# Chunk attention and a two-layer feed-forward on one core: q and k turned by transposing DMAs from the tenth group on

## The chip, the cores and the metric

The kernel runs on one core of a Trainium2 chip. The metric is the device time of one execution in microseconds (us). The kernel before took 294.09 us, the median of three runs (294.02 to 294.42).

## The reference

Attention within chunks of 64 tokens, then a feed-forward layer with a leaky ReLU. Inputs and output are float32; the kernel works in float16 with float32 sums.

```
# q, k, v: (8 batches, 8 heads, 576 tokens, 64); chunk = 64, so 9 chunks a batch
scores = (1/sqrt(64)) * matmul(q_c, k_c.T)        # per batch, head and chunk: 64 x 64
scores = scores - max(scores, axis=-1)
attn   = exp(scores); attn = attn / (sum(attn, axis=-1) + 1e-9)
x      = matmul(attn, v_c)                        # laid out as (4608 tokens, 512)
h      = x @ w_in                                 # 512 -> 2048
g      = maximum(0.01 * h, h)
out    = g @ w_out                                # 2048 -> 512
```

## The kernel before, in words

**Groups.** The 4608 tokens are taken in 36 groups of 128 tokens (two chunks), numbered u. A group crosses the border of two batches where u is 13, 22 or 31 among the later ones. Each group goes through these stages, each of which is one function that takes u:

- q and k have to stand with the head dimension on the partitions. For groups 0 to 8 (u below UD = 9) they are loaded by rows of tokens (load_qk, L59) and turned by TensorE (stage_tq L260, stage_tk L265), then copied out by VectorE and ScalarE into QZ and KT (stage_q L270, stage_k L278). For groups 9 to 35 a whole batch is loaded at a time in pieces of 32 numbers (load_qk_batch L77, issue on L86, 8 DMAs for q and 8 for k, tiles q_d and k_d, two buffers each) and VectorE turns it in 32x32 blocks (stage_dq L287 with its instruction on L290, twice a group; stage_dk L295 with its instruction on L298).
- QZ holds q of two heads on the two halves of the partitions, with zeros beside them, so that one 128-row weight load gives both heads' scores. There are three QZ buffers, used in turn.
- stage_s (L303) makes the scores Sp: 8 matmuls with 64 columns. stage_m (L315) and stage_b (L319) take the maximum and subtract it on VectorE, stage_x (L325) is the exponential on ScalarE, stage_z and stage_n (L331, L339) sum, invert and scale on VectorE, giving the tile en.
- en is turned again, by TensorE for groups 0 to 8 (stage_e, stage_c) and by a transposing DMA on SP's queue for the later ones (stage_d L359, issue on L361), giving the tile et (four buffers).
- stage_v (L365) multiplies by v, giving xp, and stage_a copies it on ScalarE into xT (L385). stage_v also starts the load of v two batches ahead (load_v, issue on L95).

**Feed-forward.** Once the tokens of a block (128, 256 or 512) stand in xT, the block is cut into pieces that the function fill(n) takes in order: mm1 (hT, matmul on L155, each piece gives one PSUM bank; ScalarE makes gT of it on L170) and mm2 (oP, matmul on L180, a piece is 4 matmuls of 512 columns). After four mm2 pieces, store (L189) copies oP to osb (three buffers) on ScalarE and issues its DMA on SP's queue (L193). hT and oP share four PSUM banks.

**Order.** The program is scheduled by hand: each engine and each queue runs its instructions in the order in which the Python issues them. The first groups follow the list FRONT. Then one loop runs over `it` from 6 to 38. Iteration `it` does the scores of group it-1, the turning of q and k of group it, and the values of an older group, with feed-forward pieces between them:

```
    for it in range(6, NU + 3):
        stage_s(it - 1); stage_m(it - 1); stage_b(it - 1)
        if dve: stage_dq(it, 0)
        fill(2)
        stage_x(it - 1)
        ...
        if dve: stage_dq(it, 1); stage_dk(it)
        ...
        stage_z(it - 1); stage_n(it - 1); stage_d(it - 1)
        fill(2)
        values(it - 3)
        fill(3 if dve and it >= 17 else 2)
        if it == 9 * b // 2 - 4: load_qk_batch(b)
```

SP's queue carries stage_d's transposing DMAs and the output stores; POOL's (GpSimd's) queue carries all casting loads from float32 to float16, issued at first by the list LOADS (L131), whose last entry D2 loads q and k of batch 2. A DMA queue is in order too: what waits at its head holds back what is behind it.

Of the kernel before, what the change touches and what calls it, by code (L numbers as in the profile page):

```python
# [8 lines left out]
FP16 = mybir.dt.float16  # L9
# [7 lines left out]
def kernel(  # L17
# [9 lines left out]
    nc = tc.nc  # L27

    B, H, S, D = q.shape
# [3 lines left out]
    CH = 64  # L33
# [1 line left out]
    NT = d_model // 128  # L35
    NFC = d_ff // 128
    SCL = float(D) ** -0.5
    NQZ = 3
    NVB = 2
    NIN = 9  # L40
    UD = 9
    G = 2 * CH

    NU = n_tok // G
    BLOCKS = [128] * 6 + [256] + [128] * 2 + [256] * 5 + [512] * 4

    sbp = ctx.enter_context(tc.tile_pool(name="k_sb", bufs=1))
# [2 lines left out]


    VB = [sbp.tile([128, H // 2, NCH, 128], FP16, name=f"VB{i}") for i in range(NVB)]
    QZ = [sbp.tile([128, 4, 2, 2, CH], FP16, name=f"QZ{i}") for i in range(NQZ)]
    w_inT = sbp.tile([128, NT, d_ff], FP16, name="w_inT")
    w_outT = sbp.tile([128, NFC, d_model], FP16, name="w_outT")
    xT = sbp.tile([128, NT, n_tok], FP16, name="xT")
    qk: dict[int, tuple[bass.AP, bass.AP]] = {}

    def load_qk(u):  # L59
# [12 lines left out]
            both.append(t)  # L72
        qk[u] = tuple(both)

    qkd: dict[int, tuple[bass.AP, bass.AP]] = {}

    def load_qk_batch(b):  # L77
        both = []
        for name, src in (("q_d", q), ("k_d", k)):
            t = sbp.tile([128, 2, 2, S // 32, 32], FP16, name=name, tag=name, bufs=2)  # L80
            for m in range(2):
                for s in range(2):
                    for dh in range(2):
                        p0 = s * 64 + dh * 32
                        h0 = 4 * m + 2 * s
                        nc.gpsimd.dma_start(  # L86
                            out=t[p0:p0 + 32, m, :, :, :].rearrange("p h b d -> p (h b) d"),
                            in_=src[b, h0:h0 + 2, :, dh * 32:dh * 32 + 32].rearrange("h (b t) d -> t (h b) d", t=32),
                        )
            both.append(t.rearrange("p m h b d -> p (m h) (b d)"))  # L90
        qkd[b] = tuple(both)

    def load_v(b):
        for m in range(2):
# [25 lines left out]
    for eng, name, src in ((nc.sync, "q_f", q), (nc.scalar, "k_f", k)):  # L120
        t = sbp.tile([128, H, D], FP32, name=name)
# [7 lines left out]
    qk[0] = tuple(sbp.tile([128, H, D], FP16, name=n, tag=n, bufs=NIN) for n in ("q_in", "k_in"))  # L129

    LOADS = (  # L131
        "g1 v0 g2 Q0 Q1 g3 Q2 Q3 g4 P0 P1 P2 P3 g5 v1 g6 g7 g8 D2 "
    )
    LOADERS = {"g": load_qk, "v": load_v, "Q": load_w_in_quarter, "P": load_w_out_quarter, "D": load_qk_batch}
    ident = sbp.tile([128, 128], FP16, name="ident")
    for n, what in enumerate(LOADS.split()):
        LOADERS[what[0]](int(what[1:]))
        if n == 0:
# [91 lines left out]
    def fill(n):  # L230
        for _ in range(n):
            if not chunks:
                return
            kind, j, a, p = chunks[0]
            if START[j] + BLOCKS[j] > state["tokens"]:
                return
            chunks.pop(0)
            if kind == "mm1":
                mm1(j, a)
                act1(j, a)  # L240
            elif j == len(BLOCKS) - 1 and a == BLOCKS[j] // 128 - 1:
                if p == 0:
                    last(j, a)
            else:
                mm2(j, a, p)
                if parts[j, a] == NFC // 4:
                    store(j, a)
# [21 lines left out]

    def stage_q(u, s, act=0):  # L270
        part = slice(s * CH, (s + 1) * CH)
        to, of = QZ[u % NQZ][part, :, :, s, :], QP[u][part]
        if act:
            nc.scalar.activation(out=to, in_=of, func=AFT.Copy, bias=0.0, scale=1.0)
        else:
            nc.vector.tensor_copy(out=to, in_=of)

    def stage_k(u):  # L278
        KT[u] = sbp.tile([128, 4, 2, CH], FP16, name="KT", tag="KT", bufs=3)
        nc.scalar.activation(out=KT[u], in_=KP.pop(u), func=AFT.Copy, bias=0.0, scale=1.0)  # L280

    def cuts(u):
        r0, r1 = u * G, (u + 1) * G
        cut = min(-(-r0 // S) * S, r1) if r0 % S else r1
        return [(a // S, a % S, (a - r0) // CH, (z - a) // CH) for a, z in ((r0, cut), (cut, r1)) if a < z]

    def stage_dq(u, s):  # L287
        qz = QZ[u % NQZ]
        for b, at, e0, n in cuts(u):
            nc.vector.transpose(  # L290
                out=qz[s * CH:(s + 1) * CH, :, e0:e0 + n, s, :],
                in_=qkd[b][0][s * CH:(s + 1) * CH, :, at:at + n * CH].rearrange("p h (e t) -> p h e t", e=n),
            )

    def stage_dk(u):  # L295
        KT[u] = sbp.tile([128, 4, 2, CH], FP16, name="KT", tag="KT", bufs=3)
        for b, at, e0, n in cuts(u):
            nc.vector.transpose(  # L298
                out=KT[u][:, :, e0:e0 + n, :],
                in_=qkd[b][1][:, :, at:at + n * CH].rearrange("p h (e t) -> p h e t", e=n),  # L300
            )

    def stage_s(u):  # L303
        qz, kt = QZ[u % NQZ], KT.pop(u)
        Sp = psp.tile([128, 8, CH], FP32, name="Sp", tag="Sp", bufs=1)
        for i in range(8):
            g, e, m = i // 4, i // 2 % 2, i % 2
            nc.tensor.matmul(  # L308
                out=Sp[:, i, :], lhsT=qz[:, 2 * m + g, e, :, :], rhs=kt[:, 2 * m + g, e, :], start=True, stop=True
            )  # L310
        SP[u] = Sp

# [53 lines left out]
    def stage_v(u):  # L366
        et = ET.pop(u)
        xp = psp.tile([128, NT, 2, CH], FP32, name="xp", tag="ox", bufs=1)
        for e in range(2):
            b, c = divmod(2 * u + e, NCH)  # L370
            for t in range(NT):
                nc.tensor.matmul(  # L372
                    out=xp[:, t, e, :],
                    lhsT=VB[b % NVB][:, t, c, :],
                    rhs=et[:, t // 2, e, t % 2, :] if u < UD else et[:, t % 2, e, t // 2, :],
                    start=True,
                    stop=True,
                )
            if c == NCH - 1 and b + NVB < B:
                load_v(b + NVB)  # L380
        XP[u] = xp
# [33 lines left out]
    def empty(i):  # L415
        i, m = divmod(i, 2)
        return VB[i][m * CH:(m + 1) * CH, :, :, (1 - m) * CH:(2 - m) * CH]

    def zero(i):
        nc.vector.memset(QZ[i] if i < NQZ else empty(i - NQZ), 0.0)  # L420

    def zero_act(i):
        to = empty(i - NQZ)
        for t in range(2):
            part = to[:, 2 * t:2 * t + 2]
            p0 = (i - NQZ) % 2 * CH
            nc.scalar.activation(
                out=part,
                in_=zeros[p0:p0 + CH].unsqueeze(2).unsqueeze(3).to_broadcast(part.shape),
                func=AFT.Copy, bias=0.0, scale=1.0,  # L430
            )
# [8 lines left out]
    )  # L440
    STAGES = {
        "tq": stage_tq, "tk": stage_tk, "q": stage_q, "k": stage_k, "s": stage_s, "m": stage_m, "b": stage_b,
        "x": stage_x, "z": stage_z, "n": stage_n, "e": stage_e, "c": stage_c, "v": stage_v, "a": stage_a,
        "A": first_layer, "G": act1, "B": second_layer, "O": finish, "i": idle, "y": zero, "w": zero_act,
        "h": cast_q, "hk": cast_k,
    }
    for what in FRONT.split():
        name = what.rstrip("0123456789.")
        STAGES[name](*(int(x) for x in what[len(name):].split(".") if x))
    def values(u):  # L450
        if 3 < u < NU:
            stage_v(u)
            stage_a(u)

    for it in range(6, NU + 3):
        dve = UD <= it < NU
        if it <= NU:
            stage_s(it - 1)
            stage_m(it - 1)
            stage_b(it - 1)  # L460
        if dve:
            stage_dq(it, 0)
        fill(2)
        if it <= NU:
            stage_x(it - 1)
        if it - 2 < UD:
            stage_e(it - 2)
            stage_c(it - 2)
        if dve:
            stage_dq(it, 1)  # L470
            stage_dk(it)
        elif it < UD:
            stage_tq(it)
            stage_tk(it)
            stage_q(it, 0)
            stage_q(it, 1)
            stage_k(it)
        if it <= NU:
            stage_z(it - 1)
            stage_n(it - 1)  # L480
            if it - 1 >= UD:
                stage_d(it - 1)
        fill(2)
        values(it - 2 if it - 2 < UD else it - 3 if it - 3 >= UD else -1)
        fill(3 if dve and it >= 17 else 2)
        for b in range(3, B):
            if it == 9 * b // 2 - 4:
                load_qk_batch(b)
    fill(len(chunks))


# [28 lines left out]
```

## Time and profile before

| what | value |
|---|---|
| median of three runs | 294.09 us (294.02 to 294.42) |
| span of the profiled execution, first to last instruction | 292.1 us |
| median less span | 2.0 us |
| granted TensorE clock | 1.000 |
| TensorE (PE) busy | 283.5 us, 97% |
| VectorE (DVE) busy | 183.8 us, 63% |
| ScalarE (ACT) busy | 155.2 us, 53% |
| GpSimd (POOL) busy, mostly issuing loads | 119.5 us, 41% |
| SP's transposing DMAs et<-en | 27 |

The profile gives a span for the profiled execution and no time of its own beside it. Sums are therefore made on the span, and the 2.0 us between it and the median, which lie outside the first and the last instruction, are carried along.

How to read it: the page's first part gives each engine's busy time, its fourth the chain of work that ended last, followed back from the end, and its fifth the costliest groups of instructions with the idle time ahead of them and what ended it. A line such as "L290 DVE STREAM_TRANSPOSE QZ<-q_d" is line 290 of the kernel, on VectorE, writing QZ from q_d. "SPq" is SP's own instruction stream, which issues DMAs; a DMA's landing is when its data has arrived.

### The profile page before, as it was taken

Reading aid. Unit: us, or ns where it says so; the run is one execution under the profiler, and the core shown is the slowest. Engines: PE = TensorE matmul, PEld = TensorE weight load, DVE = VectorE, ACT = ScalarE, POOL = GpSimd, SP = SyncE. Lnnn points to the kernel's source line nnn. Section 1 sums busy time; section 2 is a strip of 40 time slices with the busy share of each in tenths; the row PEclk is TensorE's granted clock in tenths of the full one; section 3 lists DMA queues with packets and bytes.
Section 4 is the critical chain, followed back from the end, with each engine's and each line's share of the span. In section 5 each row is a group of like instructions: output and inputs, shape, how many; then the busy total and the mean of one; then the engine's idle time right before and its main releaser. Section 6 shows DMA issues by size and latency. Waiting matters only on the chain.

```text
span 292.1 us, 6233 instructions
## 1 busy us (share of the span) xinstructions
PE 283.5 (97%) x2564; PEld 181.0 (62%) x2564; DVE 183.8 (63%) x343; ACT 155.2 (53%) x268; POOL 119.5 (41%) x148
## 2 busy tenths in 40 slices
PE   4989999999999999999999999999999999999995
PEld 4979845888677766767676744444445444444444
DVE  6987417789899998777787788778876730000000
ACT  6457623666555555646564647734873377127511
POOL 8867547998408936913295369130000000000000
PEclk9999999999999999999999999999999999999999
DMA  9999999999969999999499399999111320120022
GB/s 132 169 193 193 203 157 198 151 148 144 124 97 96 162 78 158 154 142 90 101 107 132 61 159 147 78 65 163 54 20 54 73 91 0 38 81 28 0 74 72
DMA packets 192476, 32.00 MB, mean 110 GB/s; under 512 B 183488, under 2 KB 187968, under 8 KB 192448
## 3 DMA queue, kind: packets, MB, share of 16 engines
q0 software_dynamic: 170208, 18.10, 117.7%
q1 hardware_dynamic: 21056, 13.18, 18.1%
q10 hardware_dynamic: 1184, 0.33, 0.5%
q8 instruction: 20, 0.33, 0.5%
q14 instruction: 8, 0.07, 0.1%
HBM read 36.70 MB, written 9.44 MB: 158 GB/s over the span
## 4 chain that ended last, share of the span: by engine, by line
PE 93%; DVE 3%; DMA 2%; ACT 1%; issue 1%; DVEq 0%
PE hT L155 43%; PE oP L180 41%; PE xp L372 3%; PE Sp L308 3%; DMA k_f<-in_k_dram 2%; PE oP L206 1%; PE tpe L350 1%; PE kp L268 1%; DVE mx L317 0%; DVE z L333 0%; DVE sh L321 0%; DVE en L342 0%; PE qp L263 0%; ACT ex L327 0%; DVE VB L420 0%
## 5 line engine op out<-in xcount | busy, mean ns | idle before, releaser
L155 PE MATMUL hT<-xT,w_inT 128*128 128x128 f16 (+2 forms) x1152 | 135.1, 272 | 0.2 <-issue 0.2
L180 PE MATMUL oP<-w_outT,gT 128*128 128x512 f16 x560 | 128.6, 379 | 0.0
L155 PEld LDWEIGHTS <-w_inT 128*128 128x128 f16 x1152 | 90.0, 98 | 33.4 <-issue 0.5
L170 ACT ACTIVATE gT<-hT 128x512 f16<-128x512 f32 x144 | 85.7, 596 | 34.8 <-PE hT L155 33.0
L180 PEld LDWEIGHTS <-gT 128*128 128x128 f16 x560 | 52.5, 98 | 55.8
L191 ACT ACTIVATE osb<-oP 128x512 f32<-128x512 f32 x35 | 20.9, 597 | 61.3 <-PE oP L180 58.7
L86 POOL DMA_DIRECT2D q_d<-in_q_dram x48 | 38.7, 821 | 32.0 <-DVE QZ L290 28.0
L317 DVE TENSOR_REDUCE mx<-Sp 128x8 f32<-128x512 f32 x36 | 24.9, 691 | 32.6 <-PE Sp L308 32.5
L86 POOL DMA_DIRECT2D k_d<-in_k_dram x48 | 38.7, 824 | 0.9 <-issue 0.5
L290 DVE STREAM_TRANSPOSE QZ<-q_d 64x512 f16<-64x512 f16 (+1 forms) x60 | 38.2, 644 | 0.4
L214 DVE COPY osb<-oP 128x128 f32<-128x128 f32 x1 | 0.3, 290 | 51.4 <-PE oP L206 51.4
L327 ACT ACTIVATE ex<-sh 128x512 f16<-128x512 f32 x36 | 22.5, 626 | 15.0 <-DVE sh L321 14.8
L385 ACT ACTIVATE xT<-xp 128x512 f16<-128x512 f32 x36 | 21.4, 594 | 16.4 <-PE xp L372 16.3
L95 POOL DMA_DIRECT2D VB<-in_v_dram x16 | 18.5, 1162 | 28.0 <-PE xp L372 28.0
L333 DVE TENSOR_REDUCE z<-ex 128x8 f32<-128x512 f16 x36 | 23.6, 654 | 3.9 <-ACT ex L327 3.8
L342 DVE TENSOR_TENSOR en<-ex,zi 128x512 f16<-128x512 f16 x36 | 24.9, 691 | 1.4 <-DVE zi L337 0.2
L321 DVE TENSOR_TENSOR sh<-Sp,mx 128x512 f32<-128x512 f32 x36 | 24.9, 691 | 1.2
L298 DVE STREAM_TRANSPOSE KT<-k_d 128x512 f16<-128x512 f16 (+1 forms) x30 | 19.4, 654 | 0.8
L372 PEld LDWEIGHTS <-VB 128*128 128x128 f16 x288 | 13.1, 98 | 6.8 <-issue 1.2
L308 PEld LDWEIGHTS <-QZ 128*128 128x128 f16 x288 | 13.2, 99 | 5.4 <-issue 0.3
L372 PE MATMUL xp<-et,VB 128*128 128x64 f16 x288 | 14.3, 193 | 1.1 <-DVE et L356 1.1
L308 PE MATMUL Sp<-KT,QZ 128*128 128x64 f16 x288 | 14.5, 194 | 0.2 <-ACT KT L280 0.2
(37 smaller groups left out, 112.2 us busy)
## 6 DMA issues: line engine op xcount, KB each, us to landing
out_dram<-osb SPq DMA_DIRECT2D x35, 256.0 KB, 2.3
VB<-in_v_dram POOLq DMA_DIRECT2D x16, 288.0 KB, 6.5
q_d<-in_q_dram POOLq DMA_DIRECT2D x48, 72.0 KB, 5.3
k_d<-in_k_dram POOLq DMA_DIRECT2D x48, 72.0 KB, 5.2
w_inT<-in_moe_w_in_dram POOLq DMA_DIRECT2D x8, 256.0 KB, 8.8
w_outT<-in_moe_w_out_dram POOLq DMA_DIRECT2D x4, 512.0 KB, 9.5
q_in<-in_q_dram POOLq DMA_DIRECT2D x7, 128.0 KB, 9.3
k_in<-in_k_dram POOLq DMA_DIRECT2D x7, 128.0 KB, 9.3
```

What stands on the lines that cost most here:

```text
L86: nc.gpsimd.dma_start(out=t[p0:p0 + 32, m, :, :, :].rearrange("p h b d -> p (h b) d"), in_=src[b, h0:h0 + 2, :, dh * 32:dh * 32 + 32].rear ...
L155: nc.tensor.matmul(out=hT[:, i, :], lhsT=w_inT[:, t, fc * 128:(fc + 1) * 128], rhs=xT[:, t, r0:r0 + tb], start=(t == 0), stop=(t == NT - 1),)
L170: nc.scalar.activation(out=gT[j][:, nf * a:nf * a + nf, :], in_=HT.pop((j, a)), func=AFT.Prelu, bias=0.0, scale=1.0, alpha=0.01)
L180: nc.tensor.matmul(out=o, lhsT=gT[j][:, fc, ti * 128:(ti + 1) * 128], rhs=w_outT[:, fc, :], start=(n == 0 and fc == part * 4), stop=(n == ...
L290: nc.vector.transpose(out=qz[s * CH:(s + 1) * CH, :, e0:e0 + n, s, :], in_=qkd[b][0][s * CH:(s + 1) * CH, :, at:at + n * CH].rearrange("p ...
L308: nc.tensor.matmul(out=Sp[:, i, :], lhsT=qz[:, 2 * m + g, e, :, :], rhs=kt[:, 2 * m + g, e, :], start=True, stop=True)
L317: nc.vector.tensor_reduce(out=MX[u], in_=SP[u], axis=AXL.X, op=ALU.max)
L321: nc.vector.tensor_tensor(out=SH[u], in0=SP.pop(u), in1=MX.pop(u).unsqueeze(2).to_broadcast((128, 8, CH)), op=ALU.subtract)
L327: nc.scalar.activation(out=E[u], in_=SH.pop(u), func=AFT.Exp, bias=0.0, scale=SCL)
L333: nc.vector.tensor_reduce(out=z, in_=E[u], axis=AXL.X, op=ALU.add)
L342: nc.vector.tensor_tensor(out=E[u], in0=ex, in1=ZI.pop(u).unsqueeze(2).to_broadcast((128, 8, CH)), op=ALU.mult)
L372: nc.tensor.matmul(out=xp[:, t, e, :], lhsT=VB[b % NVB][:, t, c, :], rhs=et[:, t // 2, e, t % 2, :] if u < UD else et[:, t % 2, e, t // 2, :],
```

## The change

Groups 0 to 8 are as before. From group 9 on:

- q and k are loaded by rows of tokens, one group at a time (load_rows). k goes to a tile of the shape that the first groups use. q goes into one of six tiles QI in which every head's 64 numbers have 64 places beside them, on the side that depends on the head; these places are set to zero once (zero_beside, the step Z in FRONT, 12 VectorE instructions) and never written again. A group has 3 loads, a group across two batches 6.
- stage_t issues three transposing DMAs on SP's queue: two turn the halves of QI (64 tokens by 1024 numbers each) straight into QZ, zeros included, one turns k (128 tokens by 512) into KT. stage_dq and stage_dk go, with their VectorE instructions, and so does load_qk_batch with D2.
- stage_t stands one iteration earlier than the VectorE version did: in iteration `it` it turns group it+1. Rows of groups 9 to 12 are loaded ahead of the loop, those of group it+5 at the end of iteration `it`.
- QZ has four buffers and another order of its dimensions, KT four buffers instead of three, and stage_v reads et of the later groups in the order that the first groups have.

```diff
-    NQZ = 3
+    NQZ = 4
+    NQI = 6
-    QZ = [sbp.tile([128, 4, 2, 2, CH], FP16, name=f"QZ{i}") for i in range(NQZ)]
+    QZ = [sbp.tile([128, 2, 4, 2, CH], FP16, name=f"QZ{i}") for i in range(NQZ)]
+    QI = [sbp.tile([128, 4, 2, 2, D], FP16, name=f"QI{i}") for i in range(NQI)]
+    def slot(u):
+        return u % 3 if u < UD else u % NQZ
-    def load_qk_batch(b):
...
+    def load_rows(u):
+        pad = QI[u % NQI]
+        t = sbp.tile([128, H, D], FP16, name="k_in", tag="k_in", bufs=NIN)
+        r0, r1 = u * G, (u + 1) * G
+        cut = min(-(-r0 // S) * S, r1) if r0 % S else r1
+        for a, z in ((r0, cut), (cut, r1)):
+            if a < z:
+                rows = slice(a % S, a % S + z - a)
                 for s in range(2):
+                    nc.gpsimd.dma_start(
+                        out=pad[a - r0:z - r0, :, s, s, :],
+                        in_=q[a // S, s:H:2, rows, :].rearrange("h p d -> p h d"),
+                    )
+                nc.gpsimd.dma_start(
+                    out=t[a - r0:z - r0], in_=k[a // S, :, rows, :].rearrange("h p d -> p h d")
+                )
+        qk[u] = (pad, t)
...
-        "g1 v0 g2 Q0 Q1 g3 Q2 Q3 g4 P0 P1 P2 P3 g5 v1 g6 g7 g8 D2 "
+        "g1 v0 g2 Q0 Q1 g3 Q2 Q3 g4 P0 P1 P2 P3 g5 v1 g6 g7 g8 "
...
-    def stage_dq(u, s):
-    def stage_dk(u):
+    def stage_t(u):
+        pad, rows = qk.pop(u)
+        for e in range(2):
+            nc.sync.dma_start_transpose(
+                out=QZ[slot(u)][:, e].rearrange("p i s t -> p (i s) t"),
+                in_=pad[e * CH:(e + 1) * CH].rearrange("p i a b d -> p (i a b d)"),
+            )
+        KT[u] = sbp.tile([128, 4, 2, CH], FP16, name="KT", tag="KT", bufs=4)
+        nc.sync.dma_start_transpose(
+            out=KT[u].rearrange("p i e t -> p i (e t)"), in_=rows.rearrange("p h d -> p (h d)")
+        )
...
+    def zero_beside():
+        for i in range(NQI):
+            for s in range(2):
+                nc.vector.memset(QI[i][:, :, 1 - s, s, :], 0.0)
...
-        ... A3.2 n4 G3.1 A3.3 ...
+        ... A3.2 n4 Z G3.1 A3.3 ...
+    for u in range(UD, UD + 4):
+        load_rows(u)
     for it in range(6, NU + 3):
-        if dve:
-            stage_dq(it, 0)
         fill(2)
         if it <= NU:
             stage_x(it - 1)
...
-        if dve:
-            stage_dq(it, 1)
-            stage_dk(it)
+        if UD <= it + 1 < NU:
+            stage_t(it + 1)
...
-        fill(3 if dve and it >= 17 else 2)
-        for b in range(3, B):
-            if it == 9 * b // 2 - 4:
-                load_qk_batch(b)
+        fill(3 if 17 <= it < NU else 2)
+        if 13 <= it + 5 < NU:
+            load_rows(it + 5)
```

The matmuls of all stages, their number, shapes and order on TensorE are the same in both kernels.

More of the change, by code (lines that the diff above doesn't have):

```diff
@@ L73, in load_qk @@
         qk[u] = tuple(both)
-    qkd: dict[int, tuple[bass.AP, bass.AP]] = {}
-    def load_qk_batch(b):
[L78 to L81, printed above, removed]
-                for s in range(2):
[L83 to L91, printed above, removed]
+    def load_rows(u):
[6 more added lines that the diff above has]
+                rows = slice(a % S, a % S + z - a)
+                for s in range(2):
+                    nc.gpsimd.dma_start(
[6 more added lines that the diff above has]
+        qk[u] = (pad, t)
     def load_v(b):
@@ L131 @@
     LOADS = (
-        "g1 v0 g2 Q0 Q1 g3 Q2 Q3 g4 P0 P1 P2 P3 g5 v1 g6 g7 g8 D2 "
+        "g1 v0 g2 Q0 Q1 g3 Q2 Q3 g4 P0 P1 P2 P3 g5 v1 g6 g7 g8 "
     )
-    LOADERS = {"g": load_qk, "v": load_v, "Q": load_w_in_quarter, "P": load_w_out_quarter, "D": load_qk_batch}
+    LOADERS = {"g": load_qk, "v": load_v, "Q": load_w_in_quarter, "P": load_w_out_quarter}
     ident = sbp.tile([128, 128], FP16, name="ident")
@@ L271, in stage_q @@
         part = slice(s * CH, (s + 1) * CH)
-        to, of = QZ[u % NQZ][part, :, :, s, :], QP[u][part]
+        to, of = QZ[slot(u)][part, :, :, s, :].rearrange("p e i t -> p i e t"), QP[u][part]
         if act:
@@ L278, in stage_k @@
     def stage_k(u):
-        KT[u] = sbp.tile([128, 4, 2, CH], FP16, name="KT", tag="KT", bufs=3)
+        KT[u] = sbp.tile([128, 4, 2, CH], FP16, name="KT", tag="KT", bufs=4)
         nc.scalar.activation(out=KT[u], in_=KP.pop(u), func=AFT.Copy, bias=0.0, scale=1.0)
[L282 to L285, printed above, removed]
-    def stage_dq(u, s):
[L288 to L292, printed above, removed]
-            )
-    def stage_dk(u):
[L296 to L301, printed above, removed]
+    def stage_t(u):
[4 more added lines that the diff above has]
+                in_=pad[e * CH:(e + 1) * CH].rearrange("p i a b d -> p (i a b d)"),
+            )
+        KT[u] = sbp.tile([128, 4, 2, CH], FP16, name="KT", tag="KT", bufs=4)
+        nc.sync.dma_start_transpose(
+            out=KT[u].rearrange("p i e t -> p i (e t)"), in_=rows.rearrange("p h d -> p (h d)")
+        )
     def stage_s(u):
-        qz, kt = QZ[u % NQZ], KT.pop(u)
+        qz, kt = QZ[slot(u)], KT.pop(u)
         Sp = psp.tile([128, 8, CH], FP32, name="Sp", tag="Sp", bufs=1)
@@ L308, in stage_s @@
             nc.tensor.matmul(
-                out=Sp[:, i, :], lhsT=qz[:, 2 * m + g, e, :, :], rhs=kt[:, 2 * m + g, e, :], start=True, stop=True
+                out=Sp[:, i, :], lhsT=qz[:, e, 2 * m + g, :, :], rhs=kt[:, 2 * m + g, e, :], start=True, stop=True
             )
@@ L374, in stage_v @@
                     lhsT=VB[b % NVB][:, t, c, :],
-                    rhs=et[:, t // 2, e, t % 2, :] if u < UD else et[:, t % 2, e, t // 2, :],
+                    rhs=et[:, t // 2, e, t % 2, :],
                     start=True,
@@ L419, in zero @@
     def zero(i):
-        nc.vector.memset(QZ[i] if i < NQZ else empty(i - NQZ), 0.0)
+        nc.vector.memset(QZ[i] if i < 3 else empty(i - 3), 0.0)
+    def zero_beside():
+        for i in range(NQI):
+            for s in range(2):
+                nc.vector.memset(QI[i][:, :, 1 - s, s, :], 0.0)
     def zero_act(i):
-        to = empty(i - NQZ)
+        to = empty(i - 3)
         for t in range(2):
             part = to[:, 2 * t:2 * t + 2]
-            p0 = (i - NQZ) % 2 * CH
+            p0 = (i - 3) % 2 * CH
             nc.scalar.activation(
@@ L443 @@
         "x": stage_x, "z": stage_z, "n": stage_n, "e": stage_e, "c": stage_c, "v": stage_v, "a": stage_a,
-        "A": first_layer, "G": act1, "B": second_layer, "O": finish, "i": idle, "y": zero, "w": zero_act,
+        "A": first_layer, "G": act1, "B": second_layer, "O": finish, "i": idle, "y": zero, "Z": zero_beside, "w": zero_act,
         "h": cast_q, "hk": cast_k,
@@ L453, in values @@
             stage_a(u)
+    for u in range(UD, UD + 4):
+        load_rows(u)
     for it in range(6, NU + 3):
-        dve = UD <= it < NU
         if it <= NU:
@@ L468 @@
             stage_c(it - 2)
-        if dve:
-            stage_dq(it, 1)
-            stage_dk(it)
-        elif it < UD:
+        if UD <= it + 1 < NU:
+            stage_t(it + 1)
+        if it < UD:
             stage_tq(it)
```

2 rows, old and new, of the table FRONT are left out of this document.

## The prediction

> **What bounds the kernel now.** I read the first part of the page, then the chain that ended last, then TensorE's waits, then the stretch in which the change acts.
>
> ```profile
> PE 283.5 (97%) x2564; PEld 181.0 (62%) x2564; DVE 183.8 (63%) x343; ACT 155.2 (53%) x268; POOL 119.5 (41%) x148
> ...
> PE 93%; DVE 3%; DMA 2%; ACT 1%; issue 1%; DVEq 0%
> ```
>
> TensorE is busy for 97% of the span, and the chain runs through it for 93%. VectorE's share of the chain is 3%. A busy TensorE could still hide stalls, so the list of all that it waited for comes next:
>
> ```profile
> PE idle L392 <- POOL ident masks.py:199: 3.8, 1, 3.8
> PE xp L372 <- DVE et L356: 1.1, 1, 1.1
> PE hT L155 <- issue: 0.2, 1, 0.2
> PE Sp L308 <- ACT KT L280: 0.2, 1, 0.2
> ```
>
> These are 5.3 us, all before 40 us: the same list cut to 40 us and later is empty. The iterations that turn groups 9 to 35 are seen in the table of stretches, from the scores of group 9 to those of group 35:
>
> ```profile
> 68.50:114.90 46.40, 46.40 (x486) 33.55 (x484) 42.22 (x77) 26.61 (x46) 25.91 (x32) 1.00 1.80 122
> 114.90:232.40 117.50, 117.50 (x914) 69.44 (x913) 92.02 (x168) 65.26 (x114) 42.70 (x51) 1.00 1.47 100
> ```
>
> The columns are the stretch, its length, then the busy time of PE, PEld, DVE, ACT and POOL, the granted clock, the DMA share and GB/s. TensorE is busy for 163.90 of 163.90 us at full clock. The starts of its matmuls agree: in the trace one of 512 columns follows the next after 216 ns at the median and after 217 ns at most on L180. There is nothing here for a faster VectorE to give.
>
> **What goes.**
>
> ```profile
> L290 DVE STREAM_TRANSPOSE QZ<-q_d 64x512 f16<-64x512 f16 (+1 forms) x60 | 38.2, 644 | 0.4
> ...
> L298 DVE STREAM_TRANSPOSE KT<-k_d 128x512 f16<-128x512 f16 (+1 forms) x30 | 19.4, 654 | 0.8
> ```
>
> These 57.6 us leave VectorE, 2.1 us in each of 27 iterations. An iteration lasts 6.5 us from group 16 on (scores of group 16 to those of 35: 124.0 us over 19) and 5.7 us from group 9 to 16 (39.9 over 7). En, the last VectorE result of a group, is ready 5.7 us after its scores start and should come about 0.5 to 1.3 us earlier, by the transposes that stand ahead of it. Nobody on the path waits for en: its values are multiplied 15 to 17 us after the scores. So the gain on the path is 0. On POOL 96 loads of 0.82 us (78.8 us) go.
>
> **What comes, off the path.** POOL issues 81 loads of whole groups plus 9 for the three cut ones. A k load is like the 0.88 us ones of k_in; a q half is like the halves of q_in and k_in, 0.68 us. A group costs 0.88 + 2 x 0.68 = 2.2 us of POOL's 6.5, less than before. Packets of these loads: 110,592 of 64 bytes go (each taking 27 ns at the median in the trace's packet records), 55,296 of 128 bytes come (32 ns). Over 16 DMA engines that is 187 us less and 111 us more. 81 transposing DMAs of 512 packets of 256 bytes add 47 us at the 18 ns median of such packets, 83 us at their loaded 32 ns. The sum for the DMA engines is between 29 us less and 7 us more, so they are no new bound.
>
> The 12 VectorE instructions of Z write 256 numbers each. The nearest rows are the memset of 128x1 (59 ns) and that of 128x512 (485 ns); in proportion this gives 0.16 to 0.27 us each, 2 to 3.3 us together. I take 3.3. They stand behind group 4's en and ahead of this:
>
> ```profile
> 39.81 0.86 DVE L276 COPY QZ<-qp 64x512 f16<-64x512 f16 x2 [6.23 <-PE qp L263]
> ```
>
> VectorE idles 6.2 us there until TensorE has turned group 5, so Z costs 0; without that cover it would be 3.3 us.
>
> The first rows: POOL is done with group 8 at 41.6 us. Rows of group 9 are issued in the place where q_d's first loads were (41.7 to 45.5 us) and land, by k_in's median of 8.6 us, near 54 us. Their transposes stand in the iteration that starts at 56.2 us, and the scores that need them start at 68.5 us. There are 12 us for about 9 us of issue and landing. This is not late.
>
> **What comes, on SP's queue.** This is the one place that gets tight. The nearest rows are:
>
> ```profile
> L361 SPq DMA_TRANSPOSE et<-en x27: 1189/1196/2182, 74.6 to 237.7; - x27
> ...
> DMA to landing us min/median/max: 2.4/4.4/6.5
> ```
>
> ```profile
> 81.44 0.54 SPq L193 DMA_DIRECT2D out_dram<-osb  x1
> ...
> 92.81 1.01 SPq L193 DMA_DIRECT2D out_dram<-osb  x1
> 98.95 0.33 SPq L193 DMA_DIRECT2D out_dram<-osb  x1
> ```
>
> A transposing DMA holds SP for 1.20 us; a store alone holds it 0.33 us, right behind a transposing DMA 0.54 us, and 1.01 us at worst. An iteration will issue four transposing DMAs (three of stage_t, one of stage_d) and 0.6 to 0.8 stores. The trace shows none behind another one, and none with 64 source partitions. A half of QI has the same 65,536 numbers as en, so I take 1.20 us for the first and the store's extra 0.24 us (median about 0.57, less 0.33) for each that follows: 1.20 + 3 x 1.44 = 5.5 us, with stores 5.9 us. The bounds are 4 x 1.20 = 4.8 us (no extra) and 1.20 + 3 x 1.88 = 6.8 us (extra 0.68), with stores 5.1 to 7.3 us. At my value SP is filled to 90% in the 6.5 us iterations and to 103% in the seven of 5.7 us, where it slips by 0.15 us each, 1.1 us in all.
>
> Slack decides whether that is seen. stage_t turns group it+1 in iteration `it`; the scores that need it start two iterations later, 13.0 us (or 11.4 us) after this iteration's start T. Ahead of it in the queue stands at most a store, which began up to T + 2.8 us, so stage_t begins by T + 3.4, its third DMA by T + 3.4 + 1.20 + 1.44 = T + 6.0, and it lands at T + 10.4 by the median, at T + 12.5 by the longest. That is inside 13.0. In the short iterations the store begins by T + 1.9 and the landing comes at T + 9.5, at worst T + 11.6, against 11.4. Behind stage_t wait stage_d's transposing DMA, which may be 15 us late after the scores, and the stores, held some 4 us; osb has three buffers and stores come 3.5 us apart at the fastest, so ScalarE has about 10 us until it needs the first buffer again. TensorE meets none of these.
>
> **Sum.** 0 removed from the path, 0 to 0.2 us added (the short iterations' worst landing): span 292.1 us, and with the 2.0 us that the median lies above the span, 294.1 us. A measurement of this kernel tells about 0.2% (0.6 us) from no change, and this is none.
>
> [...]
>
> **Rivals.**
>
> 1. SP's queue becomes the bound, and the kernel gets slower. It decides when the mean of four transposing DMAs passes 1.34 us in the short iterations ((5.70 - 0.33) / 4) or 1.52 us in the long ones ((6.51 - 0.42) / 4). A mean between the two costs up to 7 x 0.7 = 5 us less the slack of 1 to 2 us: 294.7 to 298 us. At the worst extra of 0.68 us (mean 1.71) it is 7 x 1.47 + 19 x 0.75 = 24.5 us, less 2 us of slack: 316 us. If a half with 64 source partitions holds SP twice as long (2.4 us), an iteration needs 7.6 us and it is about 30 us: 324 us. For it: stores do take longer behind a transposing DMA, more so while POOL loads. Against: 24 of 27 transposing DMAs in the trace took 1.19 to 1.21 us, loaded or not. Chance 0.30: 0.17 for the mild form, 0.13 for the heavy one.
> 2. [...] Chance 0.02.
> 3. Rows come too late at the start or POOL's order delays v: TensorE would wait once, 0.6 to 4 us, near 68 us. Against: 12 us of room against 9. Chance 0.04, 295 to 298 us.
> 4. The front of the kernel gets faster by other traffic of the first 40 us, where 1.5 us of TensorE's waits are not the wait for the identity. D2 starts at 41.7 us, after them, so I see no way but scatter. Chance 0.04, 293 us.
>
> **Numbers.** The forecast of 294.1 us has 0.60, its own range is 293.7 to 294.6 us. Slower by over 0.2%: 0.30 + 0.02 + 0.04 = 0.36. Faster: 0.04. The range reaches over the mild form of rival 1 and rival 3 and leaves out the heavy form, the crossbar and the lower end of rival 4, under 0.2 together: 293.6 to 300 us.
>
> **What would show it.** Right: TensorE's waits after 40 us stay empty, the stretch from the scores of group 9 to 35 stays at 163.9 us, VectorE's busy time falls by 54 us to about 130 us, SP issues 108 transposing DMAs of 1.2 to 1.5 us. Wrong: Sp on L308 waits for the DMA into KT or QZ, or VectorE or ScalarE waits for osb or et, in each iteration; or transposing DMAs over 1.5 us on SP. Least sure is the price of a transposing DMA right behind another.

## The result and the profile after

The changed kernel takes 307.16 us (median of four runs, 304.49 to 307.5) where the kernel before takes 294.17 us beside it: 4.2% slower, ratio 1.0416 with a 95% interval of 1.0372 to 1.046. The profiled execution has a span of 305.4 us against 292.1 us. The forecast was 294.1 us and no change. Single executions far above the others of the same kernel (one of 772 us of the kernel before, for instance) are left out of the ratios.

First part of the page and the chain that ended last, of the kernel after:

```profile
PE 287.3 (94%) x2564; PEld 181.0 (59%) x2564; DVE 131.7 (43%) x265; ACT 155.0 (51%) x268; POOL 111.1 (36%) x142
...
PE 65%; DMA 25%; DVE 3%; issue 2%; SPq 1%; ACT 1%; POOL 1%; DVEq 0%
```

VectorE is relieved of 52 us as meant, and DMAs now hold a quarter of the chain. All that TensorE waited for, after 68 us:

```profile
PE Sp L306 <- DMA KT<-k_in: 9.1, 6, 2.2
```

The columns are the total, the number of waits and the longest one. In six iterations the scores wait for k to be turned. The stretch from the scores of group 9 to those of group 35, of before, is 163.90 us, all of it busy. Before, and then after:

```profile
68.50:232.40 163.90, 163.90 (x1398) 102.99 (x1396) 134.24 (x245) 91.87 (x160) 68.61 (x82) 1.00 1.56 107
...
68.50:245.90 177.40, 168.31 (x1400) 103.55 (x1399) 82.32 (x157) 91.82 (x160) 64.63 (x79) 0.98 1.46 155
```

It is 13.5 us longer, which is the whole difference of the spans (13.3 us). 9.1 us of it is time in which TensorE is not busy. The other 4.4 us stand in its busy time, and the granted clock of 0.98 says why for most of it. A table of stretches around the first wait (stretch, length, busy time of PE, PEld, DVE, ACT, POOL, clock, DMA share, GB/s):

```profile
85.80:89.20 3.40, 1.28 (x25) 1.25 (x26) 0.81 (x2) 0.60 (x1) 1.02 (x2) 1.00 1.47 154
89.30:92.60 3.30, 3.30 (x9) 1.12 (x8) 2.22 (x5) 1.17 (x2) 0.87 (x2) 0.50 1.69 156
92.70:96.00 3.30, 3.30 (x49) 2.47 (x48) 0.25 (x1) 1.68 (x3) 2.22 (x3) 1.00 1.75 200
```

The wait ends at 87.9 us. From 89.3 to 92.7 us the clock is halved (0.50 in the table), and matmuls of 512 columns follow one another after 427 ns instead of 216 ns. This happens twice in the loop, for 3.41 us each time; half of that is an estimate of its cost, about 1.7 us each time, 3.4 us in all.

Why the scores wait stands in the landings of the transposing DMAs (the first DMA's row, then the landing of KT, and of et, from issue, smallest, median and largest in us):

```profile
L297 SPq DMA_TRANSPOSE KT<-k_in x27: 1189/1227/2168, 59.4 to 238.8; - x27
...
DMA to landing us min/median/max: 2.4/5.5/10.0
```

```profile
L359 SPq DMA_TRANSPOSE et<-en x27: 1195/1257/3068, 73.7 to 251.1; - x27
...
DMA to landing us min/median/max: 2.4/6.6/9.2
```

Before, et landed after 4.4 us at the median and 6.5 us at most. The chain of work around the first wait, after, in order of time (start, length, what):

```profile
76.39 1.34 SPq L292
...
77.83 9.95 DMA KT<-k_in
87.78 0.14 issue
87.92 0.39 PE Sp L306 x8
```

KT of group 12 is issued at 77.83 us, 3.4 us after the start of its iteration, earlier than the T + 5.1 us (landing at T + 9.5 less 4.4) that the prediction's working has for the short iterations. It lands 9.95 us later. The issue was on time; the landing was late. Of the six iterations with a wait this holds to within 1.1 us: the trace has KT issued 3.4 to 7.1 us after the iteration's start, where the working allows 6.0 us (5.1 in the short iterations), and landed 7.6 to 10.0 us after its issue. In the trace the 49 transposing DMAs that had, averaged over their time in flight, four or more of POOL's loads beside them landed after 7.9 us at the median, the 26 with less than half a load after 2.7 us.

### The profile page after: what moved, and what is told of

Its sections match the earlier page's. It is cut to its first block, busy times and chain, and to the rows that moved or that the text cites. A ratio compares the mean times of both kernels' runs of the same rounds, so it can differ in the third digit from the quotient of the medians.

```text
span 305.4 us, 6338 instructions
## 1 busy us (share of the span) xinstructions
PE 287.3 (94%) x2564; PEld 181.0 (59%) x2564; DVE 131.7 (43%) x265; ACT 155.0 (51%) x268; POOL 111.1 (36%) x142
## 3 DMA queue, kind: packets, MB, share of 16 engines
q0 software_dynamic: 114816, 18.10, 82.5%
q1 hardware_dynamic: 65120, 23.81, 44.3%
## 4 chain that ended last, share of the span: by engine, by line
PE 65%; DMA 25%; DVE 3%; issue 2%; SPq 1%; ACT 1%; POOL 1%; DVEq 0%
PE hT L161 30%; PE oP L186 28%; DMA KT<-k_in 16%; DMA VB<-in_v_dram 7%; PE xp L370 2%; PE Sp L306 2%; DMA k_f<-in_k_dram 2%; PE oP L212 1%; SPq L292 1%; DVE en L340 1%; DVE z L331 1%; ACT ex L325 1%; PE tpe L348 1%; POOL VB L101 1%; PE qp L269 0%
## 5 line engine op out<-in xcount | busy, mean ns | idle before, releaser
L186 PE MATMUL oP<-w_outT,gT 128*128 128x512 f16 x560 | 131.9, 386 | 0.0
L186 PEld LDWEIGHTS <-gT 128*128 128x128 f16 x560 | 53.3, 99 | 58.4 <-issue 4.3
L90 POOL DMA_DIRECT2D QI<-in_q_dram x60 | 44.3, 751 | 38.7 <-DMA QZ<-QI 17.8
L331 DVE TENSOR_REDUCE z<-ex 128x8 f32<-128x512 f16 x36 | 24.7, 685 | 34.0 <-ACT ex L325 33.9
L94 POOL DMA_DIRECT2D k_in<-in_k_dram x30 | 26.5, 882 | 0.8 <-PE oP L186 0.5
L390 PE MATMUL idle<-ident 128*128 128x128 f16 x120 | 9.3, 235 | 3.8 <-POOL ident masks.py:199 3.8
L390 PEld LDWEIGHTS <-ident 128*128 128x128 f16 x120 | 8.0, 107 | 3.8 <-POOL ident masks.py:199 3.8
```

Source lines behind the costliest of these rows:

```text
L90: nc.gpsimd.dma_start(out=pad[a - r0:z - r0, :, s, s, :], in_=q[a // S, s:H:2, rows, :].rearrange("h p d -> p h d"),)
L94: nc.gpsimd.dma_start(out=t[a - r0:z - r0], in_=k[a // S, :, rows, :].rearrange("h p d -> p h d"))
L186: nc.tensor.matmul(out=o, lhsT=gT[j][:, fc, ti * 128:(ti + 1) * 128], rhs=w_outT[:, fc, :], start=(n == 0 and fc == part * 4), stop=(n == ...
L331: nc.vector.tensor_reduce(out=z, in_=E[u], axis=AXL.X, op=ALU.add)
```

## The experiments

Theories, formed after this reading. **A**: clumps of loads in flight delay the landings, and the scores meet that latency. **B**: SP's queue cannot issue so many DMAs (the first rival). **C**: loads, stores and four transposing DMAs an iteration are together more than the DMA engines do in that time, so that something is late whatever its lead. **D**: the number of transposing DMAs alone. **E**: the turning itself is slow beside loads. In all runs of a whole kernel the kernel before ran on the same chip, at 294.0 to 294.2 us. A time without a ratio is that of a single run; the four runs of the changed kernel lie 3 us apart (304.5 to 307.5).

### One iteration more of lead

```diff
-        if UD <= it + 1 < NU:
-            stage_t(it + 1)
+        if it >= UD - 2 and it + 2 < NU:
+            stage_t(it + 2)
```

with seven QZ buffers (four for the later groups) and five of KT.

> The changed kernel with stage_t one iteration earlier (group it+2 in iteration it; four QZ buffers of their own for the later groups, five KT buffers). Theory A (the DMAs land 8 to 10 us after their issue only while clumps of loads are in flight, and the scores wait for that latency): the extra 6.5 us of lead covers the longest landing of 10 us, the 10.1 us of waits of Sp for KT fall under 1 us, no half-clock window is left in the loop, 294 to 295 us. Theory B (SP's queue cannot carry four transposing DMAs and the stores in an iteration, as my first rival said): lead helps once and the lag grows again, Sp still waits 5 us or more in all, 299 to 304 us.

Measured: 306.1 us, ratio 1.0407 (1.0391 to 1.0424). TensorE's waits:

```profile
PE xp L370 <- DMA et<-en: 9.1, 9, 2.5
```

The scores wait no more, KT is there at least 3.6 us early each time. But as much time as in the changed kernel, 9.1 us, is now lost at the values, which wait for et. In both kernels stage_d's DMA stands behind those of stage_t in the queue. Here it was issued 4.8 us after en was ready, at the median, where that is 2.1 us in the changed kernel and 0.07 us in the kernel before; and it landed after 7.1 us. KT's landings became longer too (7.1 us at the median). Theory A falls in its simple form: it forecast 294 to 295 us. Lead moves the wait from one consumer to another. Theory B forecast waits of Sp, of which there are none, but et's time in SP's queue leaves it open here. There was no half-clock window in the loop, which goes with a span 1.9 us shorter than the changed kernel's for the same wait.

### Loads one group at a time

```diff
-    NQI = 6
+    NQI = 4
```

> The changed kernel with four QI tiles instead of six, so that the rows of a group can only be loaded once the transposes four groups before have landed: the loads come one group an iteration and not three or four at once behind v. Traffic, SP's queue and lead are as in the changed kernel. Theory A (clumps of loads): KT's longest landing falls from 10.0 to about 7 us, waits of Sp fall from 9 us to under 4 us, 295 to 299 us. Theory B (SP's queue) and a theory C (total DMA traffic of an iteration is too much): nothing changes, 303 to 308 us.

Measured: 305.17 us, ratio 1.0378 (1.0326 to 1.0429), TensorE's waits for KT 8.6 us in 4, and KT's longest landing still 10.0 us. POOL now waited 84.0 us for the turned QZ, so the row loads were paced. It did not help: clumps of row loads are not the cause. The loads of v were still issued in pairs, so this run says nothing about them. This is the outcome for B and C.

### Without the row loads

```diff
-            load_rows(it + 5)
+            qk[it + 5] = held[(it + 5 - UD) % 4]
```

`held` has the tiles of groups 9 to 12.

> The changed kernel without the row loads of groups 13 to 35: these groups use the rows of groups 9 to 12 again, so their part of the output is that of other tokens. All transposing DMAs, stores and v loads stay. Theory A (loads in flight delay the landings): landings of KT at 2.5 to 4.5 us, no wait of Sp after group 16, 294 to 296 us. Theory B (SP's queue by itself): holds stay at 1.43 us in the mean, landings over 5 us and waits of Sp stay, 300 us or more.

Measured: 295.34 us, span 293.6 us. SP issues the same 108 transposing DMAs and the same stores, with holds of 1.31 us in the mean:

```profile
L297 SPq DMA_TRANSPOSE KT<-k_in x27: 1207/1257/1682, 60.4 to 226.8; - x27
...
DMA to landing us min/median/max: 2.4/2.6/7.4
```

KT's median landing falls from 5.5 to 2.6 us and one wait of 1.4 us is left, at 116 us, where theory A had forecast none. The DMAs that SP issued held it for 86.2% of the loop, against 87.5% in the changed kernel. That speaks against B, though not alone: the mean hold is now under the 1.34 us from which the first rival counted.

### Three transposing DMAs instead of four

```diff
-        for e in range(2):
+        for e in range(2 if u < UD + 4 else 1):
             nc.sync.dma_start_transpose(
```

> The changed kernel without the second of the two QI transposes for groups 13 to 35, so that half of their scores use older q. Three transposing DMAs an iteration instead of four, all loads as they are. Theory A (each transposing DMA is slow through loads): landings fall by a quarter at most, waits of Sp fall from 9 us to 2 to 5 us, 296 to 301 us. Theory B (SP's queue is just over its capacity): 3 x 1.43 + 0.42 = 4.7 us of 6.5 is far below it, waits vanish, 294 to 295 us.

Measured: 295.7 us, span 293.9 us, waits of Sp 1.6 us in 2. KT's landings are still long (6.1 us at the median, 8.6 at most), but they no longer lag into the next iteration. By time this is between the two forecasts; with the long landings and few waits it fits C: the queue is slow beside loads, and three in an iteration still get through. It does not by itself part C from B, since the run relieves SP (held for 69% of the loop) along with the DMA engines.

### Without the loads of v

```diff
-            if c == NCH - 1 and b + NVB < B:
-                load_v(b + NVB)
```

> The changed kernel without the loads of v for batches 2 to 7: their values are multiplied by the v of batches 0 and 1. The loads in flight fall by a third, POOL waits no more for xp and the row loads come paced by QI. Theory C: loads and transposes together fall back under what the DMA engines do, waits of Sp and xp under 3 us in all, 294.5 to 297.5 us. Theory D (it is the number of transposing DMAs alone, loads matter little): as the changed kernel, 300 us or more; e3 speaks against it.

Measured: 293.78 us, span 291.9 us. The stretch of the loop is again what it is before, with all four transposing DMAs and all row loads in it:

```profile
68.50:232.40 163.90, 163.90 (x1399) 102.99 (x1397) 83.00 (x157) 91.86 (x160) 50.70 (x66) 1.00 1.27 149
```

KT landed after 4.2 us at the median, 6.0 at most: close to the 4.4 and 6.5 us that the prediction had used. Taking either the row loads, or the v loads, or one transposing DMA in four away leaves at most 1.6 us of waits for DMAs. That speaks for a sum (C), against SP's queue (B; it was held for 86.3% of the loop here too) and against transposes alone (D).

### The kernel before with three more transposing DMAs

```diff
+    def stage_more(u):
+        for i in range(3):
+            nc.sync.dma_start_transpose(out=spare[(3 * u + i) % 5], in_=w_outT[:, i, :])
...
+        if UD <= it + 1 < NU:
+            stage_more(it + 1)
         if dve:
             stage_dq(it, 1)
```

> The kernel before, with VectorE's transposes, plus three transposing DMAs an iteration of 128x512 numbers each into tiles that nobody reads, where stage_t stands in the changed kernel. The computation is whole; nothing waits for the three. Theory C: et lands as late as in e1 and xp waits for it, 5 to 10 us in all, 299 to 305 us, though q and k come as before: the load on the DMA engines alone does it. If the cost came from the lead, the row loads or the new waits: 294 to 295 us.

Measured: 317.62 us, span 315.9 us, the slowest of all. TensorE's waits:

```profile
PE Sp L313 <- DVE KT L299: 18.7, 2, 10.0
```

The forecast time was too low and the place was wrong. Here not et is late but k_d: its loads land after 13.3 us at the median where they take 5.2 us in the kernel before, VectorE gets its k late, and the scores wait for VectorE, twice some 9 to 10 us, each time with a stretch of 10.2 us at half clock that begins during the wait. So the harm goes both ways: transposing DMAs on SP's queue delay the loads on POOL's queue (13.3 us instead of 5.2) just as these delay them (KT landed after 5.5 us at the median in the changed kernel, after 2.6 us without the row loads). The added DMAs alone, which nobody reads, cost 23.6 us.

### Plain copies instead of transposes

```diff
-            nc.sync.dma_start_transpose(
-                out=QZ[slot(u)][:, e].rearrange("p i s t -> p (i s) t"),
-                in_=pad[e * CH:(e + 1) * CH].rearrange("p i a b d -> p (i a b d)"),
+            nc.sync.dma_start(
+                out=QZ[slot(u)][:, e].rearrange("p i s t -> p i (s t)"),
+                in_=pad[:, :, e].rearrange("p i b d -> p i (b d)"),
             )
```

and the same for KT, from QI.

> The changed kernel with stage_t's three transposing DMAs made plain copies of as many packets of 256 bytes (QZ and KT get blocks of QI that are not turned, so the scores are of other numbers). stage_d still transposes; loads, stores and order are the same. If plain traffic on the DMA engines is what is short (theory C, with no regard to turning): landings stay near 7 us beside loads and waits of Sp and xp 5 us or more in all, 298 us or more. If the turning itself is slow beside loads (theory E): landings under 5 us, waits under 2 us, 294 to 295.5 us.

Measured: 300.87 us, span 299.1 us.

```profile
PE Sp L306 <- DMA KT<-QI: 6.1, 7, 1.6
```

Those are TensorE's waits for DMAs; the row of the copies into QZ (hold of SP, smallest, median and largest in ns):

```profile
L292 SPq DMA_DIRECT2D QZ<-QI x54: 593/608/1544, 56.5 to 230.5; - x54
```

Each copy holds SP for 0.61 us instead of 1.24, and still they land after 6.3 us (at most 9.2 us for QZ), and Sp waits seven times. Each wait is under 2 us and there is no half-clock window. The transposing DMA of et behind the copies held SP for 2.4 us at the median, so that SP was held for 77% of the loop, less than without row loads or without v, where the waits all but vanished. So E's forecast falls, and B once more: plain traffic of 256-byte packets on the DMA engines is enough for waits. Without the 3.4 us of half clock the changed kernel's span would be 302.0 us, 2.9 us more than with copies, so the turning may add something of its own; one run does not settle that.

### Versions

Four kernels load q without zeros, turn it like k and let the now idle VectorE copy the halves into QZ, whose zeros stay:

```diff
+        for to, rows in ((QT[u], q_rows), (KT[u], k_rows)):
+            nc.sync.dma_start_transpose(
+                out=to.rearrange("p i e t -> p i (e t)"), in_=rows.rearrange("p h d -> p (h d)")
+            )
...
+            nc.vector.tensor_copy(
+                out=QZ[slot(u)][part, :, :, s, :].rearrange("p e i t -> p i e t"), in_=qt[part]
+            )
```

> A whole kernel: q of the later groups is loaded by rows without zeros beside it, turned by one transposing DMA like k, and copied by two VectorE instructions into QZ, whose zeros stay from the start. Three transposing DMAs an iteration instead of four, two loads a group instead of three, lead as in the changed kernel. Theory C (with loads in flight the DMA engines do not turn 20 packets per us and engine, but about 15): 15 to 17 us of packets fit as in e4, waits of Sp at most 3 us, 294.5 to 297 us. Theory A (latency behind loads alone, whatever the number of transposing DMAs): the loads are the same, the copy takes 1 us of the lead, Sp waits 8 us or more, 302 us or more.

Measured: 296.65 us, ratio 1.0118 (1.0068 to 1.0167), waits of Sp for DMAs 1.4 us in 2. Three transposing DMAs do in a whole kernel what they did in the cut one. (Four of 512 packets each in 6.5 us are 20 packets per us for each of 16 DMA engines, three are 15.)

> e5_qcopy with stage_t one iteration earlier. Theory C: the queue keeps up on average, so the extra lead takes the last waits of Sp away: 294 to 294.8 us, no wait of TensorE after 70 us over 0.3 us. Theory A: the same, since the lead covers the latency; what separates them is e5.

Measured: 294.4 to 296.9 us over eight runs, ratio 1.0042 (1.0023 to 1.0062). The extra lead helps once the queue keeps up, but not quite to the kernel before. What waits are left in it is not shown here.

> A whole kernel: e6_qcopy_lead2 with groups 7 and 8 turned by DMA as well, which takes 16 TensorE transposes (16 x 56 ns = 0.9 us) off the path. Theory C: e6's steady state keeps, so e6's 295.1 us (median of its undisturbed runs) less 0.9 us: 293.9 to 294.6 us, about the kernel before. If SP's queue held by the wait for group 8's rows at 50 us delays stores: 295 us or more.

Measured: 294.91 us, ratio 1.0025 (1.0005 to 1.0045): 0.3 us above the forecast, and not faster than the kernel before. Its TensorE is not busy for 1.3 us of the loop:

```profile
PE xp L356 <- DMA et<-en: 0.8, 1, 0.8
...
PE Sp L292 <- DVE QZ L283: 0.4, 2, 0.2
```

> e10_early7 with three v tiles, so that a load of v waits for nothing and POOL brings the rows of the later groups at the pace at which their tiles come free, not in clumps behind v. Theory C with clumps as what makes the shortage: the last waits for DMAs go, 293.2 to 293.9 us, and less spread between runs than e6's 294.4 to 296.9. If the shortage is one of the mean and not of the clumps: as e10.

Measured: 295.58 us, ratio 1.0061 (1.0037 to 1.0085), one wait of xp for et of 1.8 us. A miss: that v waits for nothing gains nothing, which agrees with the second experiment. No version found beats the kernel before.

## Why the prediction was wrong, point by point

- **"There is nothing here for a faster VectorE to give"**: right. VectorE lost 52 us (183.8 to 131.7) and no wait of TensorE went with them. En came 5.2 us after the scores at the median instead of 5.7, the near end of the forecast, and it gained nothing on the path.
- **Z in VectorE's gap**: right. The 12 memsets took 165 ns each, 2.0 us, at the lower end of the bounds.
- **The first rows in time**: right. KT of group 9 landed at 66.0 us, its scores start at 68.5.
- **The price of a transposing DMA right behind another**, which I called least sure: about right. Holds were 1.24 us at the median and 1.43 us in the mean, between the bounds; I took 1.38.
- **"Its third DMA by T + 3.4 + 1.20 + 1.44 = T + 6.0, and it lands at T + 10.4 by the median, at T + 12.5 by the longest"**: here the sum failed. Its first half held to within 1.1 us in the six iterations that waited. Its second half did not: the landing was taken from et of the kernel before, which has the queue to itself (one in 6.5 us). As one of four, beside loads, KT landed after 7.6 to 10.0 us in these six, instead of at most 6.5. The slack that I had found, 0.5 us in the long iterations, does not cover that. The trace of before had the sign: et landed after 2.4 us at the median of the eight with none of POOL's loads in flight, after 5.0 us at the median of the nineteen beside loads.
- **"The sum for the DMA engines is between 29 us less and 7 us more, so they are no new bound"**: this is the step behind that error, and the one that failed. The packets' own times did about what I added up: the queues' shares of 16 engines went from 117.7% + 18.1% to 82.5% + 44.3%, which over the two spans is 9.5 us less. That sum is no measure of load: it fell while landings became later (et from 4.4 to 6.6 us, the stores from 2.3 to 4.8 us at the median), and shares above 100% say that the packets' times overlap. Bytes rose instead, from 107 to 155 GB/s over the loop, or from 17.5 to 27.5 MB. This could have been summed ahead: 81 transposing DMAs of 512 packets of 256 bytes are 10.6 MB.
- **Rival 1, SP's queue**: that the kernel gets slower came true, its mechanism did not, so what it has right is luck. The mean hold of 1.43 us lies between its two thresholds, where its price is 294.7 to 298 us; measured were 307.16. With as many DMAs on SP the waits all but vanish when loads go (third and fifth experiments), and they stay when each of the three holds SP half as long (copies). Threshold and price were worked out for a resource that is not the short one. A small part stays with it: in the waiting iterations KT was issued up to 1.1 us late, and with more lead et stood in SP's queue for 4.8 us.
- **Rival 2, with its chance of 0.02**: no run shows the limit that this chance, and its part of the range, was for. In the changed kernel up to six transposing DMAs were between issue and landing at once (a half of QZ was issued at 81.85 us, and KT, issued at 77.83 us, landed at 87.78 us), and the copies wait too, with landings of 6.3 against 5.7 us for QZ. In the run without row loads four turns an iteration cost nothing after 116 us.
- **What was not in the list at all**: that a wait of 2 us costs more than itself. The half clock made about 3.4 us of the 13.5.

What stays open: which limit of the DMA engines it is. Packets per us do not say it (48 per engine in the loop of before, 44 after). Bytes do order the runs: the loop moves 27.5 to 28.1 MB in the five kernels where TensorE waits 6 us or more (changed, more lead, loads one at a time, three more transposing DMAs, copies), and 17.5 to 25.1 MB in the seven others with a trace to compare, where the waits for DMAs are 1.8 us at most. That is an order and not yet a mechanism: a stretch of 3.3 us in the result's table moved 200 GB/s and the one ahead of it 156, where the mean of their loop is 155. What sets the rate is not shown: these runs do not part the loads' cast, the packets of 256 bytes and the two queues.

## What to carry to other kernels

A landing time belongs to a DMA among its neighbours: one that comes alone every 6.5 us (et before: 4.4 us at the median, 6.5 at most) says little about four in a row beside loads (KT after: 5.5 and 10.0 us), so ask what the DMA engines carry in that stretch before moving work from an idle-enough engine to them. Where several kinds of traffic ran together here, more lead only moved the wait to the next consumer (9.1 us at the scores, then 9.1 us at the values); taking bytes away (here zeros that were moved each time, a third of stage_t's packets) is what helped (307.16 to 296.65 us). And where TensorE is at its bound, as here with 163.90 us busy of 163.90 in the loop, the best that a relief elsewhere can do is nothing, so the question is only what it may put in TensorE's way.

## What the runs showed of the hardware that was not expected

- A short wait can be followed by half a clock. In the changed kernel TensorE's clock stood at 0.50 for 3.41 us after the waits of 2.2 and 2.0 us, from 1.3 us after work had resumed, and stayed at 1.00 after the four others (0.8 to 1.7 us). Its stretches at full clock were 81.92, 37.55 and 170.67 us long, which is 24, 11 and 50 times 3.41 us. In steps of that length, counted from the first moment at full clock, TensorE was idle for 2.07 and 1.96 us in the step ahead of each halving and for at most 1.17 us in any other of the loop. In other runs waits of 2.5 us (more lead) and 2.8 us (loads one at a time) left the clock at 1.00; one of 3.9 us (loads one at a time) was followed by a clock of 0.64 over 4.8 us, and the two of 8.7 and 10.0 us (three more transposing DMAs) left 0.94 over the loop. So a shorter wait can cost more than a longer one; what decides it is not shown.
- Loads issued by POOL and transposing DMAs issued by SP delay each other: three transposing DMAs an iteration on SP's queue made POOL's loads of k land after 13.3 us instead of 5.2, and KT landed after 5.5 us at the median beside the row loads, after 2.6 us without them.
- A transposing DMA into QZ holds SP for 1.24 us at the median, a plain DMA of as many 256-byte packets for 0.61 us, and beside the same loads they land after 5.7 and 6.3 us.
